# Tokens in runs of eight, late last tokens, 64-row stores and replanned loads in an attention + SoLU kernel

## The chip, the cores and the metric

The kernel runs on one core of a Trainium2 chip. The metric is the device time of one execution in microseconds; lower is better. Of the version before there are 13 runs: median 195.52 us, from 193.56 to 202.09 us. One more execution, of 195.35 us, was taken with the hardware profiler, and everything quoted below comes from it.

A core has five engines that run on their own and meet through semaphores: TensorE (PE in the profile; PEld is its loading of weights), VectorE (DVE), ScalarE (ACT), GpSimd (POOL) and SyncE (SP). Here GpSimd also issues the DMAs that load and cast, and SyncE issues the stores and the transposing DMAs.

## The reference

```python
def _attn_ref(q, k, v, g_norm):                  # q, k, v: (8, 8, 576, 64): batch, heads, tokens, head size
    kv = np.einsum('bhsd,bhse->bhde', k, v)
    out = np.einsum('bhsd,bhde->bhse', q, kv)
    rms = np.sqrt(np.mean(out * out, axis=-1, keepdims=True) + 1e-06)
    return out / rms * g_norm

def _moe_ref(x, w_in, w_out, g_ln):              # x: (4608, 512), d_ff 1024
    h = x @ w_in
    e = np.exp(h - np.max(h, axis=-1, keepdims=True))
    solu = h * e / (np.sum(e, axis=-1, keepdims=True) + 1e-09)
    mu = np.mean(solu, axis=-1, keepdims=True)
    var = np.mean((solu - mu) ** 2, axis=-1, keepdims=True)
    return ((solu - mu) / np.sqrt(var + 1e-06) * g_ln) @ w_out
```

The attention is linear (no softmax): a 64 x 64 matrix per head is made from k and v, and every q token is multiplied with it. The result, with the heads side by side, is the x of the second part. All arrays are float32 in memory.

## The kernel before

**Chunks.** The 4608 tokens are worked on in nine chunks of 512. Chunk b, for b from 0 to 7, holds the first 512 tokens of batch b; chunk 8 holds the last 64 tokens of all eight batches. A chunk goes through these stages:

- load k, v (lines 213 to 220) and q (lines 222 to 228), issued by GpSimd, with a cast to bf16. k and v come as runs of nine tokens for each of 64 partitions, two heads above each other in the 128 partitions. q comes as runs of four tokens, 1 KB of source, for each of 128 partitions and each head. The last tokens of each batch are a load of their own into `q_last` (line 231);
- kv_mm (line 291): 64 x 64 products of k and v, and copies of the result into `kvd` (lines 309 and 311) in two arrangements;
- q has to be turned so that the head size lies on partitions. For chunks 0 to 3 TensorE transposes it (line 319, and copies at lines 326 and 328); for chunks 4 to 8 one transposing DMA on SP does it (q_turn, line 333);
- o_mm (line 348): q times kv, in two halves `hf`, each with two results `z`. In chunks 0 to 7 one product has 256 columns. In chunk 8 a product is for one batch, and its 32 columns lie eight apart;
- the norm per head: square (363), mean by a product (369), reciprocal root (383 in chunk 0, 373 and 377 after it), and the product that makes x (390), on VectorE;
- h_mm (468), exp (476), u = h * e (483), squares of u (492 on ScalarE, 494 on GpSimd), sums of e in pairs (500), column sums on TensorE (534), the statistics (542 to 561);
- out_mm (582), the scaling by the row's statistic (614), and the store (623). A chunk has four blocks (c, m) of 128 tokens; one block is one DMA of 128 rows of 2 KB. The last block of chunk 8 is split by columns and stored from SP and from ACT (607).

**Order.** Nothing is scheduled by hand. Each piece of work is given to a planner (class Plan, lines 19 to 86) with an engine, a length, a rank, what it needs, and the buffers that it takes. The planner walks through time with these lengths and writes down the order in which the pieces are issued. Every engine then runs its own pieces in that order; what makes it wait on the chip are semaphores on data and buffers alone. A load of chunk b is planned behind h_mm of chunk b - 3 (line 254); `load` is the planner's estimate of what a load takes in the queue. The last tokens are planned from chunk 2 on (line 266).

**Queues.** SP runs stores and transposing DMAs in one order, POOL runs its elementwise pieces (494, 500) and the issue of loads in one order. DMAs from SP and ACT take turns on eight completion semaphores, so that one waits until the one eight before it has landed.

Of the kernel before, what the change touches and what calls it, by code (L numbers as in the profile page):

```python
# [8 lines left out]
FP32 = mybir.dt.float32  # L9
# [80 lines left out]
def kernel(  # L90
# [20 lines left out]
    nc = tc.nc  # L111
# [22 lines left out]
    def tile_of(key, shape, dtype):  # L134
        return sb.tile(shape, dtype, name=key[0] + "_sb", tag=key[0], bufs=bufs[key[0]])
# [11 lines left out]
    kvd = big.tile([128, B, 2, NP, D], BF16, name="kvd")  # L147
    q_last = big.tile([128, H, 4, D], BF16, name="q_last")
    g_rep = big.tile([128, 1], FP32, name="g_rep")
# [62 lines left out]

    def load_kv(name, src, b, hs):

        if hs.start == 0:
            T[name, b] = tile_of((name, b), [128, NP, 9, D], BF16)
        nc.gpsimd.dma_start(  # L217
            T[name, b].rearrange("p n i d -> p n (i d)")[:, hs.start // 2:hs.stop // 2],
            src[b, hs].rearrange("(n r) (p i) d -> (r p) n (i d)", r=2, i=9),
        )  # L220

    def load_q(b, hs):
        if hs.start == 0:
            T["q", b] = tile_of(("q", b), [128, H, 4, D], BF16)
        nc.gpsimd.dma_start(  # L225
            T["q", b].rearrange("p h j d -> p h (j d)")[:, hs],
            q[b, :, 0:512, :].rearrange("h (p j) d -> p h (j d)", j=4)[:, hs],
        )

    def load_q_last(b):  # L230
        nc.gpsimd.dma_start(
            q_last[b:128:B].rearrange("p h j d -> p h (j d)"),
            q[b, :, 512:S, :].rearrange("h (p j) d -> p h (j d)", j=4),
        )

# [16 lines left out]
    for b in range(B):  # L252
        at = b - 9.0 if b > 1 else (-2.0, -1.5)[b]
        behind = [] if b < 2 else [("h_mm", 0, 0)] if b == 2 else [("h_mm", b - 3, 2 if b == 3 else 0)]
        for g, hs in enumerate(heads(b)):
            part = 0.1 * g
            n = len(heads(b))
            for i, (name, src) in enumerate((("k", k), ("v", v))):
                plan.add((name, b, g), "pool", 0.75 if n == 1 else 0.6, at + part + 0.01 * i,
                         lambda name=name, src=src, b=b, hs=hs: load_kv(name, src, b, hs),  # L260
                         behind, uses=[(name, b)] if g else [],
                         first=[] if g else [(name, b)], load=2.9 / n if b < 3 else 3.5)
            plan.add(("q", b, g), "pool", 0.9 if n == 1 else 0.7, at + part + (0.02 if b < 2 else 0.1),
                     lambda b=b, hs=hs: load_q(b, hs), behind,
                     uses=[("q", b)] if g else [], first=[] if g else [("q", b)], load=2.7 / n if b < 3 else 3.3)
        plan.add(("q_last", b), "pool", 0.6, 2.0 + 0.5 * b, lambda b=b: load_q_last(b),
                 [("h_mm", 2 + b // 2, 4 * (b % 2))], load=0.5)
    for half in range(2):
# [27 lines left out]
    def kv_engine(b, x):  # L296
        return "act" if b == 1 or (b > 1 and x) else "dve"

# [14 lines left out]
    def qT_mm(c, hf, tag):  # L313

        t = T["qTp", c, hf] = bank((tag,), [128, 4, 2, 128], BF16)
        for h in range(4):
            for y in range(2):
                src = T["q", c][:, 4 * hf + h, 2 * y:2 * y + 2, :].rearrange("p z d -> p (z d)")
                nc.tensor.transpose(t[:, h, y, :], src, ident[:, :])

    def qT_copy(c, hf):
        if hf == 0:
            T["qT", c] = tile_of(("qT", c), [128, H, 2, 128], BF16)
        dst, src = T["qT", c][:, 4 * hf:4 * hf + 4], T["qTp", c, hf][:, :, :, :]
        if c == 1:
            nc.scalar.copy(dst, src)
        else:
            nc.vector.tensor_copy(dst, src)

    def q_turn(c):  # L330

        t = T["qT", c] = tile_of(("qT", c), [128, H, 2, 128], BF16)
        nc.sync.dma_start_transpose(
            t.rearrange("q h y p -> q (h y) p"), T["q", c].rearrange("p h j d -> p (h j d)")
        )

    def o_mm(c, hf, tag):

        ts = [bank((tag,), [128, 2, 2, 128], FP32) for z in range(2)]
        for z in range(2):  # L340
            T["o", c, hf, z] = ts[z]
        for pp in range(2):
            for b in [c] if c < B else range(B):
                cols = slice(0, 128) if c < B else slice(b, 128, B)
                for hh in range(2):
                    for z in range(2):
                        rows = slice(64 * z, 64 * z + 64)
                        nc.tensor.matmul(  # L348
                            ts[z][hh * 64:hh * 64 + 64, pp, :, cols], kvd[rows, b, hh ^ z, 2 * hf + pp, :],
                            T["qT", c][rows, 4 * hf + 2 * pp + hh, :, cols], start=True, stop=True,  # L350
                        )
# [23 lines left out]
    def s_exp(*i):  # L375
        t = T["rst", i] = tile_of(("rst", i), [128, 2, 2, 128], FP32)
        nc.scalar.activation(  # L377
            out=t.rearrange("p a b c -> p (a b c)"), in_=T["lss", i][:, :], func=AF.Exp, scale=-0.5, bias=zero_t[:, :]
        )

    def s_rsqrt(*i):
        t = T["rst", i] = tile_of(("rst", i), [128, 2, 2, 128], FP32)
        nc.scalar.activation(
            out=t.rearrange("p a b c -> p (a b c)"), in_=T["s", i][:, :], func=AF.Abs_reciprocal_sqrt, bias=eps_t[:, :]
        )

    def x_mul(c, hf, z):
        if (hf, z) == (0, 0):
            T["x", c] = tile_of(("x", c), [128, NP, 2, 2, 128], BF16)
        nc.vector.scalar_tensor_tensor(  # L390
            out=T["x", c][:, 2 * hf:2 * hf + 2, z], in0=T["o", c, hf, z][:, :, :, :], scalar=g_rep[:, :],
            in1=T["rst", (c, hf, z)][:, :, :, :], op0=MUL, op1=MUL,
        )
# [3 lines left out]
    for c in range(NC):  # L397
# [15 lines left out]
        if c in XBAR:  # L413
            plan.add(("qT", c), "sp", 3.5, r - 0.1, lambda c=c: q_turn(c),
                     [("q", c, 0)] if c < B else [("q_last", b) for b in range(B)],
                     uses=[("q", c)] if c < B else [], first=[("qT", c)])
        for hf in range(2):
            g = group(c, hf)
            tag = ("out", "h")[c] if c < 2 and hf else "o"
            if c not in XBAR:  # L420
                loads = [("q", c, g)] if c < B else [("q_last", b) for b in range(B)]
                qtag = "h" if c == 0 and hf else "misc"
                plan.add(("qT_mm", c, hf), "pe", 0.5, (r + w * (0.1 + 0.1 * hf)) if c else -2.0,
                         lambda c=c, hf=hf, tag=qtag: qT_mm(c, hf, tag),
                         ["ident", *loads], uses=[("q", c)] if c < B else [], first=[(qtag, "qT", c, hf)])
                plan.add(("qT", c, hf), "act" if c == 1 else "dve", 0.62 if c != 1 else 0.95, (r + w * (0.12 + 0.1 * hf)) if c else -2.0, lambda c=c, hf=hf: qT_copy(c, hf),
                         [("qT_mm", c, hf)] + ([("qT", c, 0)] if hf else []), uses=[(qtag, "qT", c, hf)] + ([("qT", c)] if hf else []),
                         first=[] if hf else [("qT", c)])
            kvs = [("kv", b, x, part) for b in ([c] if c < B else range(B)) for x in ((hf,) if b < 2 else range(2)) for part in range(3)]
            plan.add(("o_mm", c, hf), "pe", 0.25 if c < B else 1.2, r + w * (0.35 + 0.5 * hf),  # L430
                     lambda c=c, hf=hf, tag=tag: o_mm(c, hf, tag), [("qT", c) if c in XBAR else ("qT", c, hf), *kvs],
# [173 lines left out]
    def store_cols(x):  # L605
        dst = out.rearrange("(b s) (x d) -> b s x d", b=B, x=2)[:, 512:S, x, :].rearrange("b (p j) d -> j p b d", j=4)[3]
        (nc.sync, nc.scalar)[x].dma_start(dst, T["ob", NC - 1, 3][:, x])

    def scale(c, m):
# [3 lines left out]
        else:  # L613
            nc.vector.tensor_scalar_mul(out=t[:, :], in0=T["acc", c, m][:, :], scalar1=T["rstd", c][:, m:m + 1])  # L614

    def store(c, m):
        j = 2 * (m % 2) + m // 2
        if c < B:
            dst = out[c * S:c * S + 512, :].rearrange("(p j) d -> j p d", j=4)
        else:  # L620
            dst = out.rearrange("(b s) d -> b s d", b=B)[:, 512:S, :].rearrange("b (p j) d -> j p b d", j=4)

        (nc.scalar if c == NC - 1 and m % 2 else nc.sync).dma_start(dst[j], T["ob", c, m][:, :])

# [65 lines left out]
```

## Time and profile before

| | before |
|---|---|
| median of 13 runs | 195.52 us |
| lowest, highest | 193.56, 202.09 us |
| the profiled execution | 195.35 us, of which the span is 193.6 us |
| granted TensorE clock, mean of the core | 0.995 |
| PE busy | 179.5 us, 93% of the span |
| ACT busy | 141.0 us, 73% |
| POOL busy | 127.8 us, 66% |
| DVE busy | 122.3 us, 63% |
| loads by GpSimd (queue 0) | 20112 packets, 55.4% of 16 engines' span |
| stores and transposes by SP (queue 1) | 15616 packets, 21.6% |

The profile's page gives the span in 40 slices, each digit a busy share in tenths. In these lines TensorE is full from the fifteenth slice on nearly without a break, and the DMA engines are full in the first half, with short gaps:

```profile
PE   7878896998899999999999789999999999999991
...
DMA  3999999999995999699999992362111111211206
```

The times of the transposing DMAs and of the loads from issue to landing are in the view of a tile: for the transposed q they are 4.3, 7.4 and 15.5 us (least, median, most of five).

### The profile page before, as it was taken

How to read it: one execution, taken by the hardware profiler on the slowest of the kernel's cores; microseconds unless marked ns; L12 is line 12 of the kernel's file. 1: busy time of each engine (PE TensorE's matmuls, PEld its weight loads, DVE VectorE, ACT ScalarE, POOL GpSimd, SP SyncE). 2: the span in 40 equal slices, each digit the busy share in tenths (PEclk: the TensorE clock that was granted, in tenths of full speed). 3: DMA queues.
4: the chain of work that ended last, by engine and by line, in shares of the span. 5: the costliest groups of instructions: out<-in, count | busy, mean ns of one | idle time of the engine just before them, and what ended most of it. 6: DMA issues, size and time to landing. Idle time of an engine off the chain costs nothing.

```text
span 193.6 us, 5442 instructions
## 1 busy us (share of the span) xinstructions
PE 179.5 (93%) x2282; PEld 88.4 (46%) x2282; DVE 122.3 (63%) x241; ACT 141.0 (73%) x245; POOL 127.8 (66%) x136
## 2 busy tenths in 40 slices
PE   7878896998899999999999789999999999999991
PEld 2343464544354534544454335545445554544460
DVE  1346589368775888596586738577575748566450
ACT  2027888879895997899888777979789496655520
POOL 7972599500899987987797656568385838847200
PEclk9999999999999999999999999999999999999997
DMA  3999999999995999699999992362111111211206
GB/s 50 183 199 273 351 203 205 203 219 249 241 203 72 195 185 254 101 189 193 251 127 176 186 312 92 111 122 110 54 54 58 58 54 58 108 58 54 110 8 212
DMA packets 36040, 29.71 MB, mean 154 GB/s; under 512 B 11816, under 2 KB 30512, under 8 KB 36016
## 3 DMA queue, kind: packets, MB, share of 16 engines
q0 software_dynamic: 20112, 17.30, 55.4%
q1 hardware_dynamic: 15616, 11.67, 21.6%
q10 hardware_dynamic: 288, 0.39, 0.6%
q8 instruction: 18, 0.29, 0.6%
q14 instruction: 6, 0.05, 0.1%
HBM read 32.51 MB, written 9.44 MB: 217 GB/s over the span
## 4 chain that ended last, share of the span: by engine, by line
PE 62%; DMA 20%; ACT 7%; POOL 5%; DVE 2%; issue 1%; POOLq 0%; ACTq 0%
PE out_ps L582 24%; PE h_ps L468 23%; DMA q_sb<-in_q_dram 12%; DMA qT_sb<-q_sb 8%; PE misc_ps L534 4%; PE s_ps L369 3%; PE o_ps L348 2%; ACT e_sb L476 2%; POOL usq_sb L494 2%; DVE u_sb L483 1%; ACT osq_sb L363 1%; ACT lss_sb L373 1%; ACT rst_sb L377 1%; POOL v_sb L217 1%; PE misc_ps L198 1%
## 5 line engine op out<-in xcount | busy, mean ns | idle before, releaser
L468 PE MATMUL h_ps<-x_sb,w_in_sb 128*128 128x512 bf16 x276 | 70.3, 379 | 2.6 <-DVE u_sb L483 1.3
L494 POOL TENSOR_TENSOR usq_sb<-u_sb 128x512 bf16<-128x512 bf16 x50 | 52.0, 1042 | 26.4 <-DVE u_sb L483 26.3
L582 PE MATMUL out_ps<-w_out_sb,u_sb 128*128 128x512 bf16 x272 | 69.0, 379 | 0.1
L483 DVE TENSOR_TENSOR u_sb<-h_ps,e_sb 128x512 bf16<-128x512 f32 x69 | 47.3, 688 | 31.3 <-ACT e_sb L476 30.6
L500 POOL TENSOR_TENSOR es_sb<-e_sb 128x512 bf16<-128x512 f32 x36 | 45.9, 1274 | 21.7 <-ACT e_sb L476 21.3
L476 ACT ACTIVATE e_sb<-h_ps,zero_t 128x512 f32<-128x512 f32 x69 | 47.1, 684 | 11.9 <-PE h_ps L468 11.1
L468 PEld LDWEIGHTS <-w_in_sb 128*128 128x128 bf16 x288 | 27.3, 98 | 36.9 <-issue 6.2
L582 PEld LDWEIGHTS <-u_sb 128*128 128x128 bf16 x280 | 26.1, 98 | 30.9 <-issue 1.8
L363 ACT ACTIVATE osq_sb<-o_ps,zero_t 128x512 bf16<-128x512 f32 x31 | 20.1, 683 | 15.8 <-PE o_ps L348 15.8
L614 DVE TENSOR_SCALAR ob_sb<-out_ps,rstd 128x512 f32<-128x512 f32 x33 | 24.6, 745 | 9.3 <-PE out_ps L582 5.5
L390 DVE SCALAR_TENSOR_TENSOR x_sb<-o_ps,g_rep,rst_sb 128x512 bf16<-128x512 f32 x32 | 23.9, 749 | 8.5 <-ACT rst_sb L377 8.4
L377 ACT ACTIVATE rst_sb<-lss_sb,zero_t 128x512 f32<-128x512 f32 x32 | 23.3, 727 | 0.7
L373 ACT ACTIVATE lss_sb<-s_ps,eps_t 128x512 f32<-128x512 f32 x32 | 22.0, 686 | 2.1 <-PE s_ps L369 2.1
L492 ACT ACTIVATE usq_sb<-u_sb,zero_t 128x512 bf16<-128x512 bf16 x22 | 15.8, 718 | 5.4 <-DVE u_sb L483 5.3
L369 PE MATMUL s_ps<-osq_sb,head_mean 128*128 128x512 bf16 x34 | 12.9, 380 | 0.6 <-ACT osq_sb L363 0.6
L534 PEld LDWEIGHTS <-stat_sel 128*32 128x32 bf16 x720 | 10.2, 97 | 3.9 <-issue 3.8
L225 POOL DMA_DIRECT2D q_sb<-in_q_dram x10 | 8.6, 856 | 3.1 <-DMA w_in_sb<-in_moe_w_in_dram 1.5
L348 PE MATMUL o_ps<-qT_sb,kvd 64*64 64x32 bf16 (+1 forms) x240 | 8.2, 256 | 2.3 <-DMA qT_sb<-q_sb 1.8
L217 POOL DMA_DIRECT2D k_sb<-in_k_dram x10 | 7.8, 785 | 3.5 <-DMA w_in_sb<-in_moe_w_in_dram 2.0
L198 PE MATMUL s_ps<-zeros 128*128 128x512 bf16 x28 | 8.9, 436 | 1.4 <-DVE zero_t L163 1.2
L291 PEld LDWEIGHTS <-k_sb 64*64 64x64 bf16 x576 | 6.8, 107 | 4.6 <-issue 4.6
L348 PEld LDWEIGHTS <-kvd 64*64 64x64 bf16 x256 | 4.7, 114 | 8.7 <-issue 7.3
(85 smaller groups left out, 134.4 us busy)
## 6 DMA issues: line engine op xcount, KB each, us to landing
out_dram<-ob_sb SPq DMA_DIRECT2D x34, 256.0 KB, 2.9
k_sb<-in_k_dram POOLq DMA_DIRECT2D x6, 576.0 KB, 12.3
v_sb<-in_v_dram POOLq DMA_DIRECT2D x6, 576.0 KB, 12.5
q_sb<-in_q_dram POOLq DMA_DIRECT2D x6, 512.0 KB, 15.6
w_out_f<-in_moe_w_out_dram POOLq DMA_DIRECT2D x1, 2048.0 KB, 16.3
k_sb<-in_k_dram POOLq DMA_DIRECT2D x4, 288.0 KB, 11.6
v_sb<-in_v_dram POOLq DMA_DIRECT2D x4, 288.0 KB, 12.1
q_sb<-in_q_dram POOLq DMA_DIRECT2D x4, 256.0 KB, 12.0
```

Of the source, the lines that this page charges most:

```text
L363: nc.scalar.activation(out=t[:, :], in_=T[("o", *i)].rearrange("p a b c -> p (a b c)"), func=AF.Square, bias=zero_t[:, :])
L369: nc.tensor.matmul(t[:, :], head_mean[:, :], T["osq", i][:, :], start=True, stop=True)
L373: nc.scalar.activation(out=t[:, :], in_=T["s", i][:, :], func=AF.Ln, bias=eps_t[:, :])
L377: nc.scalar.activation(out=t.rearrange("p a b c -> p (a b c)"), in_=T["lss", i][:, :], func=AF.Exp, scale=-0.5, bias=zero_t[:, :])
L390: nc.vector.scalar_tensor_tensor(out=T["x", c][:, 2 * hf:2 * hf + 2, z], in0=T["o", c, hf, z][:, :, :, :], scalar=g_rep[:, :], in1=T["rst" ...
L468: nc.tensor.matmul(t[:, :], w_in_sb[:, dt, f * 128:(f + 1) * 128], T["x", c][:, dt].rearrange("p a b c -> p (a b c)"), start=(dt == 0), st ...
L476: nc.scalar.activation(out=T["e", c, f // 2][:, f % 2, :], in_=T["h", c, f][:, :], func=AF.Exp, bias=zero_t[:, :])
L483: nc.vector.tensor_tensor(out=T["u", c][:, f, :], in0=T["h", c, f][:, :], in1=T["e", c, f // 2][:, f % 2, :], op=MUL)
L494: nc.gpsimd.tensor_tensor(out=dst, in0=src, in1=src, op=MUL)
L500: nc.gpsimd.tensor_tensor(out=T["es", c][:, n, :], in0=e[:, 0, :], in1=e[:, 1, :], op=ADD)
L582: nc.tensor.matmul(T["acc", c, m][:, :], T["u", c][:, f, m * 128:(m + 1) * 128], w_out_sb[:, f, :], start=(f == 0), stop=(f == NF - 1),)
L614: nc.vector.tensor_scalar_mul(out=t[:, :], in0=T["acc", c, m][:, :], scalar1=T["rstd", c][:, m:m + 1])
```

## The change

- A q load takes runs of eight tokens, out of the nine that k and v take, in the layout of k and v: 2 KB of source for each of 64 partitions, two heads above each other. The three loads share one function. Chunk b is now made of the tokens 9p to 9p + 7 of batch b.
- The ninth tokens are chunk 8. `q_last` holds them with the batch as an inner index; a load of them is 512 runs of one token (256 bytes of source, 128 at the destination). They are planned from chunk 4 on.
- A block of 128 tokens is now twice 64 rows of the output with a pitch of nine rows, so every store is two DMAs.
- In chunk 8 a product of o_mm is for one batch again, with 64 columns that lie side by side: 64 products in place of 128.
- From chunk 5 on, the loads of chunk b are planned behind a new piece ("turned", b - 1), which lies on an engine of its own named "wait", takes 2.0 of the planner's time after q of chunk b - 1 has landed, and issues nothing.
- In chunk 1 the three copies of kv and the copy of the turned q of the second half go from ScalarE to VectorE.

```diff
-    q_last = big.tile([128, H, 4, D], BF16, name="q_last")
+    q_last = big.tile([128, NP, B, D], BF16, name="q_last")
...
-    def load_kv(name, src, b, hs):
+    def load(name, src, b, hs):
+
+        js = 8 if name == "q" else 9
         if hs.start == 0:
-            T[name, b] = tile_of((name, b), [128, NP, 9, D], BF16)
+            T[name, b] = tile_of((name, b), [128, NP, js, D], BF16)
         nc.gpsimd.dma_start(
+            T[name, b].rearrange("p n j d -> p n (j d)")[:, hs.start // 2:hs.stop // 2],
+            src[b, hs].rearrange("(n r) (p j) d -> (r p) n (j d)", r=2, j=9)[:, :, 0:js * D],
         )
...
     def load_q_last(b):
+        nc.gpsimd.dma_start(q_last[:, :, b, :], q[b].rearrange("(n r) (p j) d -> (r p) n j d", r=2, j=9)[:, :, 8, :])
...
-        behind = [] if b < 2 else [("h_mm", 0, 0)] if b == 2 else [("h_mm", b - 3, 2 if b == 3 else 0)]
+        behind = [] if b < 2 else [("h_mm", 0, 0)] if b == 2 else [("h_mm", b - 3, 2 if b == 3 else 0)] + ([("turned", b - 1)] if b - 1 in XBAR else [])
...
-        plan.add(("q_last", b), "pool", 0.6, 2.0 + 0.5 * b, lambda b=b: load_q_last(b),
-                 [("h_mm", 2 + b // 2, 4 * (b % 2))], load=0.5)
+        plan.add(("q_last", b), "pool", 0.7, 4.0 + 0.25 * b, lambda b=b: load_q_last(b),
+                 [("h_mm", 4 + b // 4, 2 * (b % 4))], load=0.7)
...
-        return "act" if b == 1 or (b > 1 and x) else "dve"
+        return "act" if (b, x) == (1, 0) or (b > 1 and x) else "dve"
...
-        if c == 1:
+        if (c, hf) == (1, 0):
             nc.scalar.copy(dst, src)
...
-            for b in [c] if c < B else range(B):
-                cols = slice(0, 128) if c < B else slice(b, 128, B)
+            n = 2 * hf + pp
+            for y in [slice(0, 4)] if c < B else range(4):
                 for hh in range(2):
                     for z in range(2):
                         rows = slice(64 * z, 64 * z + 64)
                         nc.tensor.matmul(
-                            ts[z][hh * 64:hh * 64 + 64, pp, :, cols], kvd[rows, b, hh ^ z, 2 * hf + pp, :],
-                            T["qT", c][rows, 4 * hf + 2 * pp + hh, :, cols], start=True, stop=True,
+                            ts[z][hh * 64:hh * 64 + 64, pp, y, :], kvd[rows, c if c < B else 2 * y + z, hh ^ z, n, :],
+                            T["qT", c][rows, n, y, 64 * hh:64 * hh + 64], start=True, stop=True,
                         )
...
+            plan.add(("turned", c), "wait", 2.0, r - 0.05, lambda: None, [("q", c, 0)] if c < B else [])
...
     def store_cols(x):
+        cols = slice(x * d_model // 2, (x + 1) * d_model // 2)
+        for y in range(2):
+            (nc.sync, nc.scalar)[x].dma_start(
+                rows_of(NC - 1, 1, 2 + y)[:, cols], T["ob", NC - 1, 3][64 * y:64 * y + 64, x]
+            )
...
+    def rows_of(c, z, y):
+
+        if c < B:
+            return out[c * S:c * S + S, :].rearrange("(p j) d -> j p d", j=9)[2 * y + z]
+        return out.rearrange("(b p j) d -> j b p d", p=64, j=9)[8, 2 * y + z]
...
     def store(c, m):
+
+        for x in range(2):
+            (nc.scalar if c == NC - 1 and m % 2 else nc.sync).dma_start(
+                rows_of(c, m // 2, 2 * (m % 2) + x), T["ob", c, m][64 * x:64 * x + 64, :]
+            )
```

The planner's other numbers change with it: the load of q from 2.7 and 3.3 to 2.55 and 3.2, the lengths of some pieces. What this makes of the order on the engines, in the built programs:

| engine | before | after |
|---|---|---|
| POOL: elementwise pieces ahead of the loads of chunks 5, 6, 7 | 20, 30, 40 | 21, 32, 40 |
| POOL: pieces ahead of the eight last-token loads | 20, 24, 30, 35, 40, 45, 50, 54 | 40, 42, 45, 47, 50, 53, 54, 57 |
| SP: blocks stored ahead of the transposes of chunks 4 to 8 | 4, 7, 11, 14, 18 | 4, 8, 12, 15, 20 |
| TensorE: rows in all | 4550 | 4422 |

On TensorE and ScalarE the order is the same but for the end of chunk 0 with chunk 1's second half, and for chunk 8's attention, which comes one to two blocks of four products later. On VectorE, chunk 1's second x product moves ahead of the statistics of chunk 0.

## The prediction

> **What bounds the kernel now.** I read the window table first, with the busy time of each engine in stretches of six microseconds. From 114 to 186 us TensorE has no idle time at all, at a granted clock of 1.00; from 54 to 108 us it idles 0.4 us, and just before 114 us there is one hole:
>
> ```profile
> core 0: us, PE busy (x) PEld busy (x) DVE busy (x) ACT busy (x) POOL busy (x), PEclk, DMA share, GB/s
> ...
> 102.00:108.00 6.00, 6.00 (x97) 2.93 (x96) 3.68 (x8) 5.49 (x12) 4.43 (x6) 1.00 1.28 174
> 108.00:114.00 6.00, 4.18 (x26) 1.83 (x25) 3.72 (x6) 3.85 (x7) 4.80 (x5) 1.00 1.26 260
> 114.00:120.00 6.00, 6.00 (x103) 3.09 (x101) 4.33 (x11) 5.21 (x10) 3.31 (x3) 1.00 0.67 170
> ```
>
> So in the second half a microsecond of TensorE work removed is a microsecond of span, and so is a hole filled. The waits of TensorE name the hole, and the chain shows what ends it:
>
> ```profile
> PE o_ps L348 <- DMA qT_sb<-q_sb: 1.8, 1, 1.8
> ```
>
> ```profile
> 96.40 15.52 DMA qT_sb<-q_sb
> 111.97 0.41 PE o_ps L348 x8
> ```
>
> That is T6, the transposing DMA of chunk 6 (I write Tn, kn, vn, qn for the transpose and the loads of chunk n). TensorE was ready at 110.15, T6 landed at 111.9. The other transposes landed 7.4 (T4), 13.3 (T5), 6.2 (T7) and 4.3 us (T8) after their issue, by the tile view cut to each. What differs is what was issued beside them, as the timelines of SP and POOL show:
>
> ```profile
> 61.64 1.70 SPq L333 DMA_TRANSPOSE qT_sb<-q_sb  x1
> 62.05 0.81 POOL L217 DMA_DIRECT2D k_sb<-in_k_dram  x1
> ...
> 78.57 0.83 POOL L217 DMA_DIRECT2D k_sb<-in_k_dram  x1
> 78.69 2.95 SPq L333 DMA_TRANSPOSE qT_sb<-q_sb  x1
> ...
> 96.08 0.83 POOL L217 DMA_DIRECT2D k_sb<-in_k_dram  x1
> 96.40 7.07 SPq L333 DMA_TRANSPOSE qT_sb<-q_sb  x1
> ```
>
> T4 led the next chunk's loads by 0.4 us and took 7.4. T5 and T6 trailed them by 0.1 and 0.3 us and took 13.3 and 15.5, nearly as long as the whole load (q7, issued at 97.63, landed 13.8 us later, at 111.4). T7 and T8 had no load behind them. So the lead decides.
>
> **Part 1: loads planned behind the transpose, last tokens late.** No semaphore is added: the new piece "turned" issues nothing and only moves the loads in the planner's order. In the built order POOL's loads of chunks 5, 6, 7 stand behind 21, 32, 40 of its elementwise pieces (20, 30, 40 before). On SP, T5, T6, T7, T8 stand behind one, one, one and two more stored blocks; every block is two DMAs now.
>
> k6: two more POOL pieces go first. The second, an es piece of 1.27 us, needs the e that ends at 79.34 + 0.70 = 80.04, so k6 goes out at about 81.4 instead of 78.57. T5 waits for q5 (landed at 78.6 before) and for block (1,3), scaled by 76.6; with two issues of 0.6 it can start at 77.8 to 78.7. It then leads k6 by about 3 us; by the rows of T4 and T7 it lands in 6 to 7.4 us.
>
> q6: nearest is chunk 7, where k7's issue to q7's landing took 111.4 - 96.1 = 15.3 us, with a transpose and two last-token loads inside. Without those (about 2 us for the transpose: T8's 4.3 less the 2.6 of a tiny store or load; some 0.5 for the others) it is about 13, so q6 lands at 81.4 + 13 = 94.4; at chunk 6's own 17.8 us less 2.5 it would be 96.7.
>
> T6 also waits for block (2,3): its scaling ends at 93.33 + 0.75 = 94.1, plus two issues, 95.3. k7 keeps its 40 pieces and gets one last-token load in front, 96.1 + 0.7 = 96.8. So T6 leads by 1.5 us (0.1 with the late q6), lands in 7 to 8 us at about 103, and is due at 110.15: the hole of 1.8 goes. Behind it T7 lands near 118 and is used near 129; TensorE runs into its own work. Some of the 1.8 us also let ScalarE and VectorE catch up, so I book **-1.6** (ends: -1.9, and +1.5 if T6 falls behind k7).
>
> Last tokens: each load becomes 512 runs of 128 bytes at the destination instead of 128 runs of 512. No row has such runs. The nearest, a full k load, has 512 longer descriptors and took 2.9 us of a saturated queue (k2 landed at 35.6, v2 at 38.5): that is the upper end for each, 0.5 the lower. The Trainium skill, "DMA: Bandwidth & Descriptors", Specifications, speaks against the edit: a transfer needs runs of at least 512 bytes for line rate, and shorter ones cost a read-modify-write. If all eight paid 2.9 us, the last, issued near 127.5 (three POOL pieces later than the present 123.8), would land by 134, T8 by 140. T8 is due near 145. I take **0** either way; beyond 5 us of further delay it would show one for one.
>
> **Part 2: q in runs of eight.** The descriptors of a q load halve. In the saturated queue k4, v4, q4 landed at 56.1, 58.9, 61.5: 2.8 us for 1.18 MB read, 2.6 for 1.05 MB. Both are 0.41 MB per us, so bytes set it, not descriptors; gain 0.1 per chunk. One place feels it: TensorE waits for q2 until 42.0. **-0.2** at most, booked with part 4.
>
> **Part 3: last chunk's attention.** Its 128 products of 32 strided columns become 64 of 64 contiguous ones. The weight loads give the slots:
>
> ```profile
> 54.60 0.67 PEld L291 LDWEIGHTS <-k_sb 64*64 64x64 bf16 x72 [0.42 <-issue]
> 55.31 0.76 PEld L468 LDWEIGHTS <-w_in_sb 128*128 128x128 bf16 x5
> ...
> 144.88 0.96 PEld L348 LDWEIGHTS <-kvd 64*64 64x64 bf16 x64 [0.42 <-issue]
> 145.94 0.55 PEld L582 LDWEIGHTS <-u_sb 128*128 128x128 bf16 x4
> ```
>
> 64 strided ones hold the engine for 145.94 - 144.88 = 1.06 us, 16.6 ns each; the k-v products, with the new 64 columns, 0.71 / 72 = 9.9 ns. A half is then 32 x 9.9 = 0.32 (or 0.53 if only the count tells). I take 0.4: **2 x (1.06 - 0.4) = -1.3**. Both stand where TensorE is never idle. They also move back by one or two blocks of 0.86 us; from the second to the first product that needs it there are ten blocks and two means, 9 us, one block more than now, so that chain stays hidden.
>
> **Part 4: copies of chunk 1 on VectorE.** Off ScalarE: 3 x 0.26 + 1.0 = 1.8 us. On VectorE: 3 x 0.29 + 0.69 = 1.6, partly in the 1.82 us it idled before 35.37. But in the built order the second x product now stands ahead of the statistics, 0.75 us, and rstd waits for those; the squares of the second half start at 39.0, as now. TensorE meets q2 at 42.0 whatever happens here. **0**, with 0.4 either way.
>
> **Part 5: stores of 64 rows.** Two DMAs of about 0.58 us issue for one; until the end SP has room (34 block stores, 20 us more issue in 193). At the end it has not:
>
> ```profile
> 188.98 0.54 SPq L607 DMA_DIRECT2D out_dram<-ob_sb  x1
> 189.34 0.47 ACT L603 ACTIVATE ob_sb<-h_ps,rstd 128x256 f32<-128x256 f32 x1 [1.01 <-PE h_ps L592]
> 189.84 0.56 ACTq L607 DMA_DIRECT2D out_dram<-ob_sb  x1
> ```
>
> Now they land at 188.98 + 3.3 and 189.84 + 2.6, both near 192.4. On ACT, one more issue ahead pushes the last scaling by 0.3 and one more behind it is 0.56: +0.85, less some for half the bytes. On SP the DMAs share eight completion semaphores, so with ten at the end the last one waits for the first block's second half, issued at 187.9 and landed 2.5 to 2.9 us later, 190.4 to 190.8; it lands at 193.0 to 193.7. The Trainium skill, same page, Rules for kernel authors, is against this too: two transfers to disjoint partition halves share the same engines, use one of 128 partitions. By its fixed cost of about 2.0 us per DMA the two in series cost +2; by the rows, where fixed parts overlap, +0.6 to +1.4. I take the rows: **+1.0**.
>
> **Sum**: -1.6 - 1.3 + 1.0 + 0 = -1.9. The profiled execution took 195.35 (span 193.6 and 1.75 around it), so 193.45; it lies 0.2 under the median 195.52. I say 193.5.
>
> **Rivals.** (a) T6 lands as now, because nothing on the chip holds POOL back: k7 is issued when 40 pieces are done, lead or not. For it: the 96.7 above. Then -1.3 + 1.0 = -0.3: 195.1. (b) Slower: T6 becomes later than now, as it waits for a q6 issued 2.8 us later and for block (2,3), with k7 in front unmoved. It decides once T6 is issued after k7, near 97; at 98 with 15.5 us it lands at 113.5, the hole is 3.35, +1.5 against now, and the sum +1.5 - 1.3 + 1.0 = +1.2: 196.5. Against it: chunk 7's 15.3 us, and the last-token loads gone from in front. (c) Inside the forecast: tail +0.6, products -1.5, hole -1.9, q2 -0.2: 192.3.
>
> **Chances.** Forecast with (c) 0.66, (a) 0.18, (b) 0.16. The forecast's own range is 192.2 to 194.5; to hold 8 in 10 it reaches to 196.2. What a measurement here can tell from no change is about 0.5%, 1 us. Faster by more 0.64, within 0.19, slower 0.17.
>
> **What would show it.** T5 and T6 landing in under 9 us, each issued ahead of the next k; no TensorE wait for qT_sb near 110; slots of the last chunk's products near 0.4 us; an end about 1 us longer from the last product. If T6 trails k7, or SP's last store waits beyond 191, the forecast is too low; a hole at T8 would break it.

## The result and the profile after

The changed kernel took 193.04 us (median of 11 runs, 192.65 to 200.66), the kernel before 195.51 us beside it (median of 48 runs). The ratio is 0.990, with a 95% interval of 0.987 to 0.993. Run again on another occasion, as the first experiment, it gave 0.991 (0.988 to 0.994). Ratios leave out executions more than 1.5% above a kernel's fastest. Here these are part of the story: 2 of the 11 runs took 200 us, and 8 of the 20 later ones 197 to 200, so the ratio tells the gain of the good executions alone.

Two profiles of the changed kernel show both outcomes. I begin with the later one, an execution of 192.84 us with a span of 190.9. The window table has the columns of before:

```profile
102.00:108.00 6.00, 6.00 (x97) 3.02 (x97) 4.34 (x9) 5.55 (x12) 5.45 (x6) 1.00 1.16 211
108.00:114.00 6.00, 6.00 (x52) 2.56 (x53) 3.88 (x7) 5.39 (x10) 5.75 (x7) 1.00 1.38 195
114.00:120.00 6.00, 6.00 (x106) 3.03 (x95) 4.13 (x10) 4.91 (x10) 3.48 (x4) 1.00 0.93 177
```

The first number behind the length is TensorE's busy time. The 4.18 of before in the middle row is now 6.00: the hole is gone. The timelines of SP and POOL show what stands where T6 trailed k7 before:

```profile
78.82 1.62 SPq L320 DMA_TRANSPOSE qT_sb<-q_sb  x1
80.63 0.81 POOL L218 DMA_DIRECT2D k_sb<-in_k_dram  x1
...
94.99 1.72 SPq L320 DMA_TRANSPOSE qT_sb<-q_sb  x1
96.21 0.76 POOL L218 DMA_DIRECT2D k_sb<-in_k_dram  x1
```

T5 leads k6 by 1.8 us and lands 3.7 us after its issue (13.3 before). T6 leads k7 by 1.2 us and lands in 4.6 (15.5 before). The weight loads of chunk 8's first products show their slot:

```profile
144.92 0.33 PEld L335 LDWEIGHTS <-kvd 64*64 64x64 bf16 x32 [0.42 <-issue]
145.30 0.55 PEld L457 LDWEIGHTS <-w_in_sb 128*128 128x128 bf16 x4
```

From 144.92 to 145.30 is 0.38 us, where it was 1.06; the second half takes 152.35 to 152.72, 0.37. The end of SP and of ACT:

```profile
183.56 2.53 SPq L617 DMA_DIRECT2D out_dram<-ob_sb  x4
186.18 1.19 SPq L597 DMA_DIRECT2D out_dram<-ob_sb  x2
```

```profile
184.58 1.22 ACTq L617 DMA_DIRECT2D out_dram<-ob_sb  x2
185.93 0.47 ACT L592 ACTIVATE ob_sb<-h_ps,rstd 128x256 f32<-128x256 f32 x1 [1.38 <-PE h_ps L581]
186.43 1.25 ACTq L597 DMA_DIRECT2D out_dram<-ob_sb  x2
```

TensorE's last product ends at 185.53, the span at 190.9: 5.37 us, where it was 193.6 - 189.30 = 4.30 (189.30 is where the last product of before ends). So the span fell by 2.7 us, and these differences make it up: 0.66 before T6 is due (chunk 5's first product stands at 93.43 instead of 94.09), 1.8 for the hole, 2 x 0.68 = 1.36 for chunk 8's products, less 1.07 at the end.

The other profile, taken with the first result, is of an execution of 199.33 us with a span of 197.6. Timelines, waits of TensorE, window table:

```profile
96.72 0.76 POOL L218 DMA_DIRECT2D k_sb<-in_k_dram  x1
97.42 9.47 SPq L320 DMA_TRANSPOSE qT_sb<-q_sb  x1
```

```profile
PE o_ps L335 <- DMA qT_sb<-q_sb: 4.4, 1, 4.4
```

```profile
108.00:114.00 6.00, 2.00 (x10) 0.79 (x8) 2.96 (x5) 2.12 (x4) 5.69 (x6) 1.00 1.39 183
114.00:120.00 6.00, 5.58 (x25) 2.22 (x25) 1.45 (x2) 3.43 (x6) 0.03 (x1) 0.72 1.32 259
```

Same program, same order: q6 landed at 97.4 instead of 94.5, so T6 went out 0.7 us behind k7, took 17.0 us, and TensorE stood for 4.4. In the next window it was granted 0.72 of its clock on the mean (1.00 in the execution above). Cut finer, that is half of the clock for 3.4 us:

```profile
114.70:118.10 3.40, 3.40 (x15) 1.20 (x9) 0.75 (x1) 1.87 (x3) 0.00 (x0) 0.50 1.35 257
118.10:120.00 1.90, 1.90 (x10) 0.88 (x9) 0.69 (x1) 1.56 (x3) 0.03 (x1) 1.00 1.35 226
```

So this execution is a race between T6 and k7, lost. The others near 200 us have no profile; that they lost the same race fits, but isn't shown. The kernel before has runs of both kinds too: of its 33 beside the first four experiments, 5 took 193.7 us or less.

### The profile page after: what moved, and what is told of

It reads as the page before. It is cut to its first block, busy times and chain, and to the rows that moved or that the text cites. A ratio compares the mean times of both kernels' runs of the same rounds, so it can differ in the third digit from the quotient of the medians.

```text
span 197.6 us, 5356 instructions
## 1 busy us (share of the span) xinstructions
PE 180.2 (91%) x2218; PEld 88.0 (45%) x2218; DVE 123.4 (62%) x245; ACT 140.1 (71%) x241; POOL 128.5 (65%) x136
## 4 chain that ended last, share of the span: by engine, by line
PE 68%; DMA 12%; ACT 8%; DVE 3%; POOL 3%; issue 2%; ACTq 1%; POOLq 0%
PE out_ps L571 26%; PE h_ps L457 25%; DMA qT_sb<-q_sb 9%; PE misc_ps L523 4%; DMA v_sb<-in_v_dram 4%; PE s_ps L356 3%; ACT e_sb L465 2%; PE o_ps L335 2%; ACT osq_sb L350 2%; DVE u_sb L472 1%; ACT lss_sb L360 1%; POOL k_sb L218 1%; ACT rst_sb L364 1%; PE misc_ps L278 1%; DVE w_out_sb L562 1%
## 5 line engine op out<-in xcount | busy, mean ns | idle before, releaser
L457 PE MATMUL h_ps<-x_sb,w_in_sb 128*128 128x512 bf16 x276 | 71.2, 383 | 2.6 <-DVE u_sb L472 1.3
L571 PE MATMUL out_ps<-w_out_sb,u_sb 128*128 128x512 bf16 x272 | 69.8, 383 | 0.0
L335 PE MATMUL o_ps<-qT_sb,kvd 64*64 64x256 bf16 (+1 forms) x176 | 6.9, 250 | 4.9 <-DMA qT_sb<-q_sb 4.4
L198 PE MATMUL s_ps<-zeros 128*128 128x512 bf16 x28 | 9.6, 469 | 1.4 <-DVE zero_t L163 1.2
L296 DVE CAST kvd<-misc_ps 64x128 bf16<-64x128 f32 (+1 forms) x27 | 7.7, 286 | 3.0 <-PE misc_ps L278 2.8
L218 POOL DMA_DIRECT2D q_sb<-in_q_dram x10 | 7.5, 750 | 3.0 <-DMA w_in_sb<-in_moe_w_in_dram 1.3
## 6 DMA issues: line engine op xcount, KB each, us to landing
q_sb<-in_q_dram POOLq DMA_DIRECT2D x6, 512.0 KB, 14.5
```

The costliest lines, as they stand in the source:

```text
L457: nc.tensor.matmul(t[:, :], w_in_sb[:, dt, f * 128:(f + 1) * 128], T["x", c][:, dt].rearrange("p a b c -> p (a b c)"), start=(dt == 0), st ...
L571: nc.tensor.matmul(T["acc", c, m][:, :], T["u", c][:, f, m * 128:(m + 1) * 128], w_out_sb[:, f, :], start=(f == 0), stop=(f == NF - 1),)
```

## The experiments

Each kernel was timed beside the kernel before. The theory after the result was the prediction's own: the loads planned behind the transpose give T6 its lead. Rivals: the late last tokens do, or the new layout of q.

**The changed kernel again.**

> The changed kernel once more, beside the kernel before on the same chip. Theory (the predicted sum): about 2 to 2.5 us faster than before; in an undisturbed profile T5 and T6 each lead the next chunk's k load and land in under 9 us, TensorE does not wait for qT_sb near 110 us, the two slots of the last chunk's attention products are near 0.4 us each (1.06 before), and the end is about 1 us longer. Rival (T6 still lands as before): a wait of 1.5 us or more for qT_sb stays in every profile, and the gain comes from the products and from somewhere not named.

Measured: 193.24 us (192.34 to 200.18, 20 runs), ratio 0.991 (0.988 to 0.994). Its profile is the first one above.

**Before, with only the loads planned behind the transpose.**

```diff
+ ... + ([("turned", b - 1)] if b - 1 in XBAR else [])
+            plan.add(("turned", c), "wait", 2.0, r - 0.05, lambda: None, [("q", c, 0)] if c < B else [])
```

> The kernel before with the planning of loads behind the transpose alone; everything else as before, and POOL's loads of chunks 5, 6, 7 then stand behind 21, 32, 40 pieces as in the changed kernel, T5, T6, T7 behind 8, 12, 15 blocks. If the order of loads fills the hole at T6: about 1.6 us faster than before (193.9), no wait for qT_sb. If the hole was filled by other parts (late last tokens, shorter q loads): no faster than before, within 0.5 us.

Measured: 198.39 us (197.76 to 199.10, 6 runs), ratio 1.020 (1.014 to 1.027): slower. Over all runs the medians are 198.39 and 195.27, 1.6% apart. Timelines and TensorE's wait:

```profile
96.72 0.80 POOL L217 DMA_DIRECT2D k_sb<-in_k_dram  x1
98.01 9.14 SPq L333 DMA_TRANSPOSE qT_sb<-q_sb  x1
```

```profile
PE o_ps L348 <- DMA qT_sb<-q_sb: 4.1, 1, 4.1
```

k6 went out at 81.47, as planned, but q6 landed only at 97.9, and k7 had moved by just 0.6 us. T6 trails by 1.3 us, lands at 114.3, and the hole grows from 1.8 to 4.1. By itself this part does the opposite of what the forecast booked for it.

**The changed kernel without it.**

```diff
-        behind = ... + ([("turned", b - 1)] if b - 1 in XBAR else [])
+        behind = ...
```

> The changed kernel without the planning behind the transpose: loads of chunks 5, 6, 7 behind 20, 30, 40 pieces again. If the order of loads fills the hole: about 1.6 us slower than the changed kernel, T5 and T6 beside the loads and 13 to 15 us long. If the late last tokens and larger runs do it: as fast as the changed kernel.

Measured: 192.99 us (192.20 to 195.87, 14 runs, 12 of them under 194.1), ratio 0.992 (0.988 to 0.996).

```profile
78.10 0.81 POOL L218 DMA_DIRECT2D k_sb<-in_k_dram  x1
...
93.84 3.27 SPq L320 DMA_TRANSPOSE qT_sb<-q_sb  x1
96.36 0.81 POOL L218 DMA_DIRECT2D k_sb<-in_k_dram  x1
```

k6 goes out as early as in the kernel before, T6 leads k7 by 2.5 us, no run took 196 or more. The gain doesn't need the planning. My theory fell here. Taken out, "turned" even seems to cost: the means of all runs, beside each other, are 195.84 us before, 195.40 with it and 193.31 without it. In the profiles with it k6 goes out 2.5 to 3 us later and q6 lands at 94.5 or 97.4 instead of 92.6, while k7 hardly moves (96.2 and 96.7, 96.4 without), so less of the lead is left.

**One store of 128 rows per block.** The rows of the output land in another order within a chunk here, so that one plain DMA stores a block.

```diff
-        for x in range(2):
-            (...).dma_start(rows_of(c, m // 2, 2 * (m % 2) + x), T["ob", c, m][64 * x:64 * x + 64, :])
+        dst = out[c * 512:c * 512 + 512, :].rearrange("(p j) d -> j p d", j=4)[m]
+        (...).dma_start(dst, T["ob", c, m][:, :])
```

> The changed kernel with one DMA of 128 rows for each block (pitch of four rows as before; the rows land in another order, so the output is permuted and nothing else is left out). Measures part 5. Predicted: 1.0 us faster than the changed kernel (0.6 to 1.4), all of it in the time after the last product. Rival (doubling the stores costs nothing at the end or gains by smaller pieces): within 0.4 us of the changed kernel.

Measured: 197.18 us (6 runs: one of 191.69, the others 196.5 to 198.6). That is 4 us over the changed kernel, where 1 us under it was expected. The span of its profile is 195.0. T6 trailed k7 by 0.3 us there, took 16.6 and left a hole of 3.7. The end is what was asked: the last product ends at 188.71 + 1.91 = 190.62, so 4.38 us, one less than with two stores. The run of 191.69 lies 1.1 under the 192.8 or so of the changed kernel's good ones.

**Before, with late last tokens alone.**

```diff
-        plan.add(("q_last", b), "pool", 0.6, 2.0 + 0.5 * b, ..., [("h_mm", 2 + b // 2, 4 * (b % 2))], load=0.5)
+        plan.add(("q_last", b), "pool", 0.6, 4.0 + 0.25 * b, ..., [("h_mm", 4 + b // 4, 2 * (b % 4))], load=0.5)
```

> The kernel before with one part of the change: the last-token loads planned from chunk 4 on instead of chunk 2 (their layout and the runs of q stay as before). In the built order no last-token load stands ahead of the loads of chunks 5, 6, 7 any more, where two to four did. Theory L (the hole before chunk 6's products went because the loads of chunk 6 no longer queue behind last tokens of 512 longer descriptors, so q6 lands earlier): T6 leads k7 and lands in under 8 us, no TensorE wait for qT_sb, 195.3 - 1.8 = 193.5. Theory Q (it went because a q load has half the descriptors): T6 still trails k7, hole near 1.8 us, 195.3.

Measured: 195.19 us (193.49 to 201.30, 12 runs), ratio 0.998 (0.993 to 1.004): no change that can be told. The profiled execution is a bad one, of 201.3 us. T5 and k6 went out 0.14 us apart; T5 took 12.8 us, k6 14.3 (7.1 before); q6 landed at 100.8. T4, 0.09 us behind k5, took 16.4.

**The changed kernel with early last tokens** (the same lines the other way round).

> The changed kernel with the last-token loads planned from chunk 2 on, as before. Loads of chunks 5, 6, 7 stay behind 21, 32, 40 pieces of POOL, with one last-token load ahead of k5 and three or four ahead of k7. Theory L: q6 lands later by what the loads ahead take (1 us or more), T6 trails k7 in most executions, hole of 2 to 4 us, 195 to 197.5. Theory Q: as the changed kernel, 193.2, T6 leading by about 1 us.

Measured: 193.35 us (192.83 to 199.84, 12 runs, 8 of them under 193.6), ratio 0.991 (0.986 to 0.995). T6 was issued at 96.31, k7 at 96.56: a lead of 0.25 us, and T6 landed in 8.0. Late last tokens aren't what the gain needs either.

**Layout, products, stores and copies alone:** both planning edits undone, so that loads, transposes and stores stand in the order of before.

> The changed kernel without the piece that holds loads behind the transpose and with the last tokens planned from chunk 2 on: the order of loads, transposes and stores is exactly that of the kernel before, and what is left is the layout (q in runs of eight, last-token runs of 128 bytes, 64-column products), the 64-row stores and the copies of chunk 1. Theory L: T6 trails k7 as before, hole of about 1.8 us; 195.3 - 1.36 (products) + 1.07 (end) - 0.35 (first half of chunk 0) = 194.6. Theory Q: no hole, 192.8, and q loads that land 1 us or more earlier after their k.

Measured: 194.36 us (12 runs, six from 192.67 to 193.38 and six from 195.34 to 197.24), ratio 0.993 (0.988 to 0.999). The profile, of an execution of 193.38:

```profile
77.96 0.80 POOL L218 DMA_DIRECT2D k_sb<-in_k_dram  x1
...
93.10 4.10 SPq L320 DMA_TRANSPOSE qT_sb<-q_sb  x1
95.76 0.81 POOL L218 DMA_DIRECT2D k_sb<-in_k_dram  x1
```

From the issue of k6 to the landing of q6 are 15.1 us, where it was 17.8 in the profile of before with the same order around it. T6 leads by 2.7. So without either planning edit T6 has the lead in this execution, and half of the runs are as fast as it; the median lies near the 194.6 of "theory L", the good half near the 192.8 of "theory Q". Which of the parts that are left gives the lead was not taken apart: no kernel has the new layout of q alone, or the 64-row stores alone.

**Is it the number of descriptors of q?** Two kernels, both on the version without "turned", with each q load in two DMAs. One splits the heads and keeps runs of eight, the other splits the tokens into runs of four, which doubles the descriptors (packets of the load queue 19248 and 23344).

```diff
+ two DMAs:  T["q", b][:, half of the heads]  <-  src[..., 0:8 * D]
+ or:        T["q", b][:, x]                  <-  src[:, :, x * 256:x * 256 + 256]   for x in range(2)
```

> The control for the next kernel: the changed kernel without the piece that holds loads behind the transpose (loads of chunks 5, 6, 7 behind 20, 30, 40 pieces of POOL), and each q load issued as two DMAs, the first for half of the heads, the second for the other half. The runs stay at eight tokens, so the descriptors of a q load are as many as in the changed kernel; only one issue of POOL, about 0.76 us, is added per chunk. Both theories: q6 lands 14 to 15.5 us after the issue of k6, T6 leads k7 by 1 us or more, no TensorE wait for qT_sb, 193.0 to 193.8.

> The same, but the two DMAs of a q load take tokens 0 to 3 and 4 to 7 of all heads: runs of four tokens, so the descriptors of q are twice as many, as in the kernel before; issues and order are those of the control. Theory Q (the descriptors of q set when q6 lands beside the transpose): q6 lands 17 us or more after the issue of k6, T6 is issued near or behind k7 in half of the executions or more, hole of 2 us or more where it trails, median 195 or more, at least 1.5 us over the control. Rival (bytes set it, or the layout with two heads above each other rather than the length of a run): as the control within 0.5 us.

Measured: 196.69 us (196.18 to 198.29) and 196.99 us (196.36 to 199.01), 12 runs each; ratios 1.010 (1.006 to 1.014) and 1.006 (1.002 to 1.010). T6 was issued at 95.17 and 95.41, 13.6 and 13.7 us after k6, and landed in 5.2 and 4.4. Twice the descriptors: 0.1 us from k6's issue to T6's in the profiles; the medians lie 0.3 apart, the ratios the other way. In the saturated queue of the first half it is more. With k4 issued at 39.7 and 39.8, q4 landed at 60.3 with the heads split and at 61.5 with the tokens split. The old layout has 61.6 to 61.9 in its three profiles, the new one 60.4 to 60.9 in its eight with whole q loads. So there twice the descriptors cost about 1.2 us by q4, for which TensorE doesn't wait at chunk 4. For T6 the pair missed its aim, since the extra issues held k6 and k7 back so far that no transpose was near a load (T6 led by 3.9 and 3.8), and both took 3 us more than expected. Waits of TensorE, heads split:

```profile
PE h_ps L526 <- POOL es_sb L492: 2.4, 1, 2.4
PE h_ps L359 <- POOL osq_sb L349: 1.3, 1, 1.3
```

Neither wait is this long in the kernel without the split. In chunks 0 and 1 a q load has two issues already, so there are four more of some 0.7 us there, and POOL's pieces behind them are on TensorE's path.

**Part 4 undone.**

```diff
-        return "act" if (b, x) == (1, 0) or (b > 1 and x) else "dve"
+        return "act" if b == 1 or (b > 1 and x) else "dve"
-        if (c, hf) == (1, 0):
+        if c == 1:
```

> The changed kernel with part 4 undone: the three copies of kv and the copy of the turned q of chunk 1's second half on ScalarE. If part 4 is worth nothing: 193.2. If it is the 0.3 us by which TensorE was earlier from chunk 1 to chunk 2 in the changed kernel: 193.5, and the first product of chunk 2 at about 43.7 instead of 43.3.

Measured: 193.64 us (6 runs, four from 192.67 to 193.73, two at 196.5 and 197.5), ratio 0.984 (0.977 to 0.992; the kernel before took 196.25 us on this occasion, 195.27 beside the first four, so 0.984 is not to be set against 0.991). Chunk 2's first product stands at 43.63. It stood at 43.34 in the changed kernel but at 43.62 in the one without "turned", which has the copies on VectorE. From the first weight load of chunk 1's products to it are 11.99 us here, and 12.15 to 12.39 in the seven profiles that have part 4 and whole q loads. So part 4 is worth nothing that shows. T6 led k7 by 0.07 us and took 11.1.

**One DMA per block, to the right rows.** Two ways. The first gives the two groups of 64 rows to one DMA as its outer dimension:

```diff
-        for x in range(2):
-            (...).dma_start(rows_of(c, m // 2, 2 * (m % 2) + x), T["ob", c, m][64 * x:64 * x + 64, :])
+        (...).dma_start(rows_of(c, m // 2, 2 * (m % 2)), T["ob", c, m][:, :])
...
-            return out[c * S:c * S + S, :].rearrange("(p j) d -> j p d", j=9)[2 * y + z]
+            return out[c * S:c * S + S, :].rearrange("(p j) d -> j p d", j=9)[2 * y + z:2 * y + z + 3:2]
```

> The changed kernel without the piece that holds loads behind the transpose, and with every block stored by one DMA of 128 rows again, to the same rows of the output (two groups of 64 rows as two dimensions of one DMA). If the second DMA of a block costs what part 5 says (1.07 us at the end, by the traces of before and after), and the loads stay as in the kernel without that piece (T6 leading k7 by 2.5 us): 193.0 - 1.0 = 192.0, the end after the last product near 4.3 us. If T6 falls behind k7, as in the run with permuted rows: 196 or more. If what made the end longer was not the number of DMAs: 193.0.

Measured: 293.72 us (6 runs), ratio 1.507 (1.498 to 1.516). The DMA view from 220 to 280 us, where nothing but stores of blocks is left in the queues, shows kind, packets, MB and the share of sixteen engines:

```profile
DMA packets 1521, 3.11 MB, mean 52 GB/s; under 512 B 20, under 2 KB 20, under 8 KB 1518
...
q1 hardware_dynamic: 1392, 2.81, 12.0%
```

12% of sixteen engines is about two engines. The DMA moves 256 KB as ever, but at 52 GB/s, 5 us for a block, and the stores hold up everything behind them. Two is the size of the outer dimension.

The second way makes the run of four tokens the inner dimension of the rows, by the pitch with which o_mm writes its result:

```diff
-        ts = [bank((tag,), [128, 2, 4, 64], FP32) for z in range(2)]
+        ts = [bank((tag,), [128, 2, 64, 4], FP32) for z in range(2)]
-                            ts[z][hh * 64:hh * 64 + 64, pp, y, :], ...
+                            ts[z][hh * 64:hh * 64 + 64, pp].rearrange("p q y -> p y q")[:, y], ...
...
+            return out[c * S:c * S + S, :].rearrange("(p j) d -> p j d", j=9)[ps, z:8:2]    # ps: 32 of the 64 p
```

> A version with one DMA of 128 rows per block that does not have two groups of 64 rows: the kernel without the piece that holds loads, and the products of o_mm written to PSUM so that the four tokens 2y + z of a run lie side by side (a pitch of 16 bytes in the write). A block is then 32 partitions' runs of four rows, 128 rows with the run as the outer dimension, stored by one DMA. If the second DMA of a block costs 1.1 us at the end, and the strided write of PSUM costs nothing: 193.0 - 1.1 = 191.9, the end 4.3 us after the last product. If a product with a strided write takes 10 % longer (128 of 270 ns on the path): +3.5. If the division of a DMA over the engines follows the outer dimension (32 here, 2 in the run with one DMA of two groups), stores land 2.6 to 3.3 us after issue at the end; if not, as slow as there.

Measured: 193.20 us (193.10 to 193.38, 6 runs), ratio 0.984 (0.978 to 0.990). The groups of its products:

```profile
L335 PE MATMUL o_ps<-qT_sb,kvd 64*64 64x256 bf16 x112 | 8.9, 408 | 0.5 <-ACT qT_sb L313 0.5
L335 PE MATMUL o_ps<-qT_sb,kvd 64*64 64x64 bf16 x64 | 1.3, 243 | 0.0
```

A product of 256 columns written with a pitch of 16 bytes takes 408 ns, where it took 280. The last product ends at 185.88 + 1.91 = 187.79, 1.77 later than in the kernel without "turned" (186.02), and the end is 191.5 - 187.79 = 3.71 us instead of 5.38. What the stores give, the products take: 1.67 and 1.77. The median is the changed kernel's, but here none of six runs is slow as from a lost race; T6 led by 2.0 us in its profile. With 32 as the outer dimension the stores are not slow (they land in 2.0 to 2.4 us). A version with these stores and without the strided write was not tried.

**T6 over all runs.** One profiled execution each, without the kernel whose stores ran at 52 GB/s; lead is k7's issue less T6's, the time is from T6's issue to its landing, both in us:

| kernel | lead of T6 | T6 takes | hole of TensorE at T6 |
|---|---|---|---|
| before | -0.3 | 15.5 | 1.8 |
| before, loads planned behind | -1.3 | 16.3 | 4.1 |
| before, late last tokens | -3.8 | 14.1 | 3.9 |
| changed, first profile | -0.7 | 17.0 | 4.4 |
| changed, permuted rows | -0.3 | 16.6 | 3.7 |
| changed, copies on ACT | 0.1 | 11.1 | none |
| changed, early last tokens | 0.25 | 8.0 | none |
| changed, second profile | 1.2 | 4.6 | none |
| interleaved rows | 2.0 | 3.7 | none |
| changed, without "turned" | 2.5 | 6.8 | none |
| layout and stores alone | 2.7 | 9.0 | none |
| tokens split, heads split | 3.8, 3.9 | 4.4, 5.2 | none |

T4 against k5 and T5 against k6, where the same profiles have their landings, say the same with a less sharp edge: 0.1 us behind they took 13.3 and 16.4 us, 0.14 ahead 12.8, 0.4 to 1.0 ahead 5.0 to 8.0, more than 1.5 ahead 3.7 to 6.2.

## Why the prediction was right, and where it was not

The forecast was 193.5, and 193.04 was measured. Its sum of -1.9 stands against -2.7 in the spans. The place of the hole, the products and the end were read rightly. That the largest term came out is in part luck: the hole was filled, but not by what the forecast gave as the cause. By its own steps:

- **"The lead decides."** Borne out by all thirteen profiles: with a lead of T6 over k7 it lands in 3.7 to 11.1 us and TensorE doesn't wait; behind k7 it takes 14.1 to 17.0, and TensorE waits 1.8 to 4.4. No run moves the lead and nothing else; the two profiles of the one changed kernel (1.2 ahead, 4.6 us; 0.7 behind, 17.0 us) come nearest. A lead of 0.1 us, the forecast's case with the late q6, is not safe: 0.07 gave 11.1 us for T6, 0.14 gave 12.8 for T5.
- **Part 1, the numbers.** They came out in the good executions: k6 at 81.4 (80.63), q6 landed at 94.4 (94.5), T6 at 95.3 (94.99), k7 at 96.8 (96.21), the hole of 1.8 gone. Booked were -1.6; as T6 landed about 10 us before it was due, all of the 1.8 came.
- **Part 1, the cause.** This step failed. "k6: two more POOL pieces go first" was the start of the chain, and the forecast took the 13 us from k6's issue to q6's landing as what is left of chunk 7's 15.3 once transpose and last tokens are out of the way. In the old layout with that part alone (T5 0.9 us ahead of k6, a last-token load on each side) it was 16.5, and T6 lost. Without that part, in the new layout, T6 won with k6 as early as before. What the runs show in its place is that each planning edit alone does not bring the gain, and that layout and stores in the old order bring part of it (0.993), with half of the runs at 195.3 or more. What makes q6 land earlier isn't settled. From k6's issue to q6's landing are 16.5 to 22.4 us in the three profiles of the old layout and 13.9 to 16.3 in the eight of the new one with whole q loads; but one program alone spreads from 13.9 to 16.3. The number of descriptors by itself makes 0.1 us at chunk 6 where no transpose is near. That the old layout suffers more beside a transpose would fit chunk 6 (17.8 us with T5 issued 0.1 behind k6, 15.1 and 14.5 in the new with T5 0.1 and 0.4 behind), but chunk 5 speaks against it: with T4 issued 0.4 to 0.6 us ahead of k5, k5's issue to q5's landing took 16.6 in the old layout, 16.6 and 16.9 in the new.
- **Rival (b)** is no mere thought. Its case, T6 at 98 with 15.5 us and a hole of 3.35, is the kernel before with "turned" alone (98.01, 16.3, 4.1), and some of the changed kernel's own runs. What it lacked is the price of the clock: there too the granted clock is 0.73 on the mean of the six microseconds behind the hole (0.50 for 3.4 of them), 6 x 0.27 = 1.6 us of work. With the hole's 2.3 that about makes the 3.7 us by which the span (197.3) exceeds that of before.
- **Last tokens at 0.** Held: T8 was issued at 131.18 and landed at 136.3, 8.6 us before its product at 144.92. The price that the forecast weighed for runs under 512 bytes doesn't show where the queue is otherwise empty: behind 116 us the loads with 128-byte runs landed in 2.7 to 3.2 us, the one of before with 512-byte runs in 3.1.
- **Part 2 at -0.2 at most, booked as 0.** Too little. Chunk 2's first product stands at 43.92, 44.10 and 44.17 in the three profiles of the old layout, and at 43.11 to 43.84 in eight of the new (means 44.06 and 43.55). That is 0.5 us, and it stays where the copies are back on ScalarE, so it is not part 4. It goes with q2, which lands at 41.7 to 42.0 in the old layout and at 41.0 to 41.6 in the new, 2.1 to 2.5 us ahead of the product. "Bytes set it, not descriptors" was the step that failed: by q4 the pair with split loads shows 1.2 us for twice the descriptors in the saturated queue. How much of q2's share is descriptors (0.3 in that pair), and how much the shorter issue, isn't shown.
- **Part 3 at -1.3.** Measured 1.36; a slot of 0.4 was taken, 0.38 and 0.37 are there.
- **Part 4 at 0.** Held.
- **Part 5 at +1.0.** Measured 1.07 in the changed kernel, 1.0 against the one with permuted rows. The place was half right. ACT's chain accounts for it: the last scaling ends 0.36 us later after the last product (0.3 forecast), and two issues follow for one, 0.69 more. SP's wait on a completion semaphore isn't seen. Its last two issues start 0.09 us after the four before them end: SP was short of issue time, not of semaphores. The fixed cost in the Trainium skill ("DMA: Bandwidth & Descriptors", Anatomy of one DMA — SWDGE (gpsimd) path; about 2.0 us for each DMA that GpSimd issues), taken in series for these stores of SP and ACT, would have given twice too much. Two stores from one queue overlap all but their issue here, about 0.6 us.

## What to carry to other kernels

When two queues race for the same engines, look at the lead in several executions, not at the median: a kernel whose lead is about as large as the spread of its landings (here 1.2 us against 2.4) has two times, and an edit that moves the first load without the second may turn the lead round. Test each edit of a bundle alone and taken out alone; here a bundle of 0.990 held a part that is 1.020 by itself, and the bundle without it had no run at 196 us or more in 14, against 8 in 20. A DMA split in two costs its issue on the engine whose issue ends last, about 0.6 us each, and more where that engine's next piece is awaited.

## What the runs showed of the hardware

- A transposing DMA is sensitive to what is issued within a fraction of a microsecond of it: 0.25 us ahead of a load of 576 KB it took 8.0 us, 0.14 ahead 12.8, 0.07 ahead 11.1, 0.1 behind 13.3, 0.3 behind 15.5.
- The granted clock stays at 1.00 through TensorE's hole of 1.8 us. Behind holes of 3.7, 4.1 and 4.4 us it is 0.50 for 3.4 us, behind one of 3.9 us (late last tokens) 0.50 for 6.8 us.
- A DMA of 128 rows whose outer dimension is two used 12% of sixteen engines, about two of them, at 52 GB/s. With an outer dimension of 32, the same bytes landed in 2.0 to 2.4 us at the end of the kernel.
- In the saturated queue of the first half, q loads with 1 KB runs of source landed later than those with 2 KB runs: q4 at 61.5 instead of 60.3 us, with the same bytes and the same number of issues.
- A 64x64x256 product that writes PSUM with a pitch of 16 bytes takes 408 ns instead of 280.
